# Attention scores of two groups in one step on eight 32x64 tiles, with a new order of the later steps

## The chip, the core and the metric

The kernel runs on one core of a Trainium2 chip. The metric is the device time of one execution in microseconds (us). Before the change three runs took 194.02, 194.83 and 199.41 us; the median, 194.83 us, is the time that counts. Every time below that is not one of these three comes from the profile of one execution of the same kernel.

## The reference

Inputs are q, k and v of 8 batches, 8 heads, 576 positions and head width 64, and four weight matrices. Attention is taken within chunks of 64 positions; a phase-mixing block follows on the concatenated heads:

```python
scores = scale * np.matmul(q_c, k_c.transpose(0, 1, 2, 4, 3))   # chunks of 64 x 64
attn = np.exp(scores - max); attn = attn / sum
x = np.matmul(attn, v_c)                       # (8, 576, 512) after the heads are joined
theta = x @ w_theta
zr, zi = x * np.cos(theta), x * np.sin(theta)
y = einsum('ts,bsd->btd', w_tok_r, zr) + einsum('ts,bsd->btd', w_tok_i, zi)
u = x + y
out = u + np.maximum(u @ w_ch, 0.0)
```

All arithmetic on the core is in fp16 operands with fp32 sums; inputs and the output in HBM are fp32.

## The kernel before, in words

**Work units.** The batches go in four pairs p = 0 to 3. A pair has nine tiles of 128 positions, j = 0 to 8: 0 to 3 of its first batch, 4 to 7 of its second, and tile 8 (MID), which joins the last 64 positions of both. For the attention the tiles are handled in groups: A (tiles 0, 1), B (2, 3), C (4, 5), D (6, 7) and M (tile 8).

**The order is a list written out by hand.** `ORDER` is a string of steps such as `S.2A.1`: the kind of step, then the pair and the group (or tile), then the slots or PSUM banks that it uses. A loop at the end of the kernel walks the list and calls one function for each step; every engine executes its own instructions in that order, and semaphores hold an instruction back until its inputs are there. So the list decides, for each engine and each DMA queue, what stands behind what.

**The kinds of step that matter here**, with the lines of the kernel before:

- `qk` (L167) loads q and k of a group, two DMAs of 256 KB on chip (L179; for M four of 64 KB, L174); `v` (L219) loads v of a group into `v16`, 256 KB in three DMAs (L233; M: 128 KB in two); `lw`, `lp`, `lc` load weights. All these are issued by GpSimd (POOL) in list order. They convert fp32 to fp16 on the way.
- `T` (L291) transposes q and k in 32x32 blocks on VectorE (L286).
- `S` (L334) makes the scores on TensorE: `score_mms` (L319) issues, for each of 8 heads, 2 halves e of the head width and 4 row quarters c, one matmul of 32 rows by 64 columns (L325): 64 for a full group, 32 for M, whose group has two quarters alone. A matmul works on one tile of the array: the quarter c gives its 32 rows, and the half `to` of the output gives its 64 columns. Of the eight such tiles a group uses four, one in each row quarter.
- `E` (L350) is the exponential on ScalarE, `V0`, `V1` (L376) the product with v for heads 0 to 3 and 4 to 7 on TensorE, in 64x64 tiles (L389): 16 matmuls for a full group, 8 for M. `N0`, `N1` (L398) divide by the sums on VectorE.
- `X` transposes x on TensorE (L421) and `xa`, `xv` copy the result; `xd` instead lets a DMA transpose x (L433). `H` is theta (L449), `G` cosine and sine on ScalarE, `Z` the products zr and zi on VectorE.
- `Y` is the token mix, nine matmuls of 128x128 by 512 for a tile (L528; for tile 8 eighteen in 128x64 tiles), `A` adds x, `U` with `ua`/`uv` or `ud` (DMA transpose, L563) turns u, `W` is the channel product (L573), `R` the relu and sum on VectorE (L578), and `st`, `sa`, `sg` store a tile of the output (256 KB) from the queue of SyncE (SP), ScalarE or GpSimd (L672). All `xd` and `ud` are issued by SP, in list order with the `st`.

**Where chunks lie.** The second tile of a group has its two chunks of 64 positions swapped in the partitions of v and of the exponentials (`crossed`, L215), except in groups A and B of pair 0. `load_v`, `score_mms` and `attn` all follow it. So the four score tiles of a group lie at column halves 0, 1, 1, 0 in the row quarters 0 to 3.

**Time around the change.** TensorE starts at 9.0 us, ends its last product at 187.7 us, and is seldom idle in between; loads are issued until 104.6 us, and the first transposing DMA and the first store are issued at 100.1 and 101.6 us.

Of the kernel before, what the change touches and what calls it, by code (L numbers as in the profile page):

```python
# [17 lines left out]
on.00 init.00 qk1.0A.0 pre.00 qk0.0A.1 qk.0B.2 cy0.0A.3 cv1.0A qk.0M.4 T0.0A.1 S0.0A.0 Tq.0B.0  # L18
v.0A Tk.0B v.0M v.0B Tq.0M.5 lw.03.2 S.0B.2 T1.0A E0.0A.0 V0.0A.0 Tk.0M S1.0A.4 E1.0A S.0M.6
lp.00 E.0M.1 V0.0M.7 N0.0A V1.0M.6 qk.0C.4 N1.0M V1.0A.4 dm.2.0 E.0B.2 lw.01.5 V1.0B.2 V0.0B.0  # L20
N1.0A X.0A.4 qk.1M.1 lw.02.3 N1.0B N0.0B xa.0A.1 X.0B.5 TW.03.3 v.0C N0.0M X.0M.7 xv.0B.2
H1.0A.5 G1.0A.0 H1.0B.0 G1.0B.3 xv.0M.4 Tq.0C.2 Z1.0A H0.0A.7 qk.0D.0 lw.00.6 G0.0A.1 v.0D
twv.03 Z0.0A H.0M.5 H0.0B.4 G.0M.4 TW.01.6 G0.0B.1 Ya.03.3 Tk.0C S.0C.0 Z1.0B twv.01 v.1M E.0C.3
Z0.0B Ya.01.6 Yb.01 TW.02.4 twa.02 Z.0M Ym.01 T.1M.2 A.01 Yb.03 V0.0C.0 Ym.03 V1.0C.4 Tq.0D.1
S.1M.6 E.1M.4 Ya.02.7 Yb.02 Ym.02 N1.0C Tk.0D S.0D.4 N0.0C A.03 TW.00.0 qk.1B.2 A.02 X.0C.3
lw.04.0 E.0D.3 U.01.6 ua.01.0 U.02.4 ua.02.1 U.03.5 twv.00 Ya.00.0 V1.0D.6 uv.03.2 qk.1A.6
xv.0C.1 N1.0D V0.0D.4 H.0C.2 G.0C.1 qk.1D.3 V0.1M.6 N0.0D X.0D.4 xv.0D.3 v.1B N0.1M Z.0C Yb.00
v.1A Ym.00 v.1D H.0D.4 Ya.05.2 T.1B.4 G.0D.5 V1.1M.3 A.00 Ya.06.6 TW.04.0 S.1B.4 Ya.04.7 N1.1M
X.1M.3 E.1B.4 Z.0D Yb.06 T.1A.4 Ym.06 S.1A.4 qk.1C.6 A.06 Yb.05 T.1D.5 xv.1M.3 U.06.6 twv.04
E.1A.1 Ym.05 Ya.07.4 V1.1B.0 qk.2M.3 A.05 ua.06.3 N1.1B V0.1B.5 N0.1B Yb.04 lc.00 S.1D.2 v.1C  # L30
V1.1A.0 Yb.07 qk.2C.5 Ym.07 qk.2D.4 N1.1A E.1D.2 V0.1D.2 N0.1D X.1B.0 xa.1B.4 V1.1D.5 Ym.04
H.1M.1 H.1B.2 qk.2B.0 N1.1D V0.1A.5 A.07 qk.2A.2 qk.3B.1 Y.08.4 T.1C.7 A.04 N0.1A X.1A.5 U.04.6
G.1M.2 Z.1M xv.1A.1 U.00.7 S.1C.0 v.2M G.1B.6 E.1C.4 A.08 X.1D.5 xv.1D.2 v.2B W.06.2 R.06.3
U.07.0 H.1A.4 uv.04.3 V0.1C.2 v.3D uv.07.4 v.2A uv.00.5 W.00.7 G.1A.7 N0.1C U.05.0 U.08.6
uv.08.5 v.2C V1.1C.2 W.01.1 uv.05.6 H.1D.4 N1.1C X.1C.2 Z.1A Z.1B R.01.2 qk.3A.6 W.08.3 xa.1C.4
Y.10.0 H.1C.1 G.1D.7 Z.1D T.2M.8 T.2A.7 W.02.4 S.2M.5 v.3B G.1C.9 Z.1C R.02.4 E.2M.1 Y.13.6 A.13
T.2B.9 S.2A.1 W.04.4 R.00.0 Y.16.5 qk.3D.0 R.04.5 R.08.6 W.05.4 S.2B.6 T.2D.7 E.2B.7 T.2C.2
Y.11.3 A.11 R.05.8 A.16 W.03.6 R.03.9 Y.15.7 A.15 E.2A.10 V1.2A.5 A.10 S.2C.3 E.2C.11 V0.2M.1
N0.2M V1.2M.7 N1.2M Y.14.2 N1.2A V0.2B.3 N0.2B V0.2A.0 V0.2C.6 v.2D Y.17.5 A.14 A.17 V1.2C.2
N1.2C N0.2A N0.2C Y.18.4 xd.2C.12 S.2D.2 st.04 qk.3M.2 V1.2B.0 E.2D.1 X.2A.5 W.07.6 N1.2B v.3C  # L40
V0.2D.0 R.07.7 N0.2D V1.2D.2 xa.2A.11 v.3A X.2M.7 X.2B.5 v.3M Y.12.6 A.12 N1.2D H.2A.0 xa.2M.10
A.18 T.3A.7 H.2M.6 xa.2B.1 G.2M.13 T.3D.5 Z.2M H.2C.4 H.2B.6 G.2A.6 xd.2D.5 ud.16.4 G.2C.0 Z.2C
ud.17.2 T.3B.9 H.2D.0 W.17.4 S.3D.2 G.2D.4 Z.2D ud.11.6 W.11.5 R.17.5 R.11.13 sa.06 ud.14.3
# [12 lines left out]
Y.33.4 A.33 st.15 ud.36.4 W.36.7 W.23.3 R.27.5 ud.38.2 sg.35 sa.34 R.23.13 R.36.1 W.38.6 R.38.0  # L56
sa.37 sa.28 Y.30.4 Wp.31.6.7 uv1.31 sa.38 A.30 W0.31 ud.32.3 W.32.1 R0.31.7 sa0.31 R.32.6 U.30.6
sa.36 W1.31 uv.30.1 R1.31 st.27 ud.33.6 W.33.4 R.33.0 st.32 sa.33 W.30.6 sg.23 dm.2.7 R.30.13
st1.31 sa.30
""".split()  # L60


@with_exitstack
def kernel(
# [11 lines left out]
    nc = tc.nc  # L76
    B, H, S, D = q.shape
# [670 lines left out]
```

## Time and profile before

| what | value |
|---|---|
| three timed runs | 194.02, 194.83, 199.41 us |
| span of the profiled execution, first to last instruction | 191.7 us |
| median of the runs less that span | 3.1 us |
| TensorE busy (matmul) | 173.9 us, 91% |
| TensorE weight loads | 91.1 us, 48% |
| VectorE busy | 138.8 us, 72% |
| ScalarE busy | 81.4 us, 42% |
| GpSimd busy (mostly issuing loads) | 88.4 us, 46% |
| DMA packets | 103338, 31.86 MB |

The profile gives the span of its execution and no other clock for it; what lies around the span is known only as the difference to the runs. A busy TensorE is not TensorE at its peak: matmuls overlap, so the record of one is longer than the time after which the next one starts. The chain of work that ended last gives the time from the start of a step to the start of the next; that is the price used below.

### The profile page before, as it was taken

Reading aid. Unit: us, or ns where it says so; the run is one execution under the profiler, and the core shown is the slowest. Engines: PE = TensorE matmul, PEld = TensorE weight load, DVE = VectorE, ACT = ScalarE, POOL = GpSimd, SP = SyncE. Lnnn points to the kernel's source line nnn. Section 1 sums busy time; section 2 is a strip of 40 time slices with the busy share of each in tenths; the row PEclk is TensorE's granted clock in tenths of the full one; section 3 lists DMA queues with packets and bytes.
Section 4 is the critical chain, followed back from the end, with each engine's and each line's share of the span. In section 5 each row is a group of like instructions: output and inputs, shape, how many; then the busy total and the mean of one; then the engine's idle time right before and its main releaser. Section 6 shows DMA issues by size and latency. Waiting matters only on the chain.

```text
span 191.7 us, 5957 instructions
## 1 busy us (share of the span) xinstructions
PE 173.9 (91%) x2579; PEld 91.1 (48%) x2579; DVE 138.8 (72%) x255; ACT 81.4 (42%) x100; POOL 88.4 (46%) x125
## 2 busy tenths in 40 slices
PE   0168899999999999999999969999999999999992
PEld 0155455645554655554555425454444444455450
DVE  0564789879779977996885968396686677553782
ACT  3113895476629946803218659142032560400000
POOL 8998289697798955799878000000000001100110
PEclk9999999999999999999999999999999999999999
DMA  5999999999999999999999986497356894885667
GB/s 159 202 157 182 188 132 143 164 177 165 151 153 183 175 182 181 157 116 152 164 133 132 196 145 168 82 197 222 74 158 126 112 281 103 246 230 150 180 173 259
DMA packets 103338, 31.86 MB, mean 166 GB/s; under 512 B 94672, under 2 KB 99152, under 8 KB 103312
## 3 DMA queue, kind: packets, MB, share of 16 engines
q0 software_dynamic: 76048, 17.33, 98.2%
q1 hardware_dynamic: 23872, 9.57, 23.9%
q10 hardware_dynamic: 3392, 4.59, 7.6%
q8 instruction: 20, 0.33, 0.7%
q14 instruction: 6, 0.05, 0.1%
HBM read 33.06 MB, written 9.44 MB: 222 GB/s over the span
## 4 chain that ended last, share of the span: by engine, by line
PE 78%; DMA 8%; DVE 4%; POOL 4%; issue 2%; ACT 1%; DVEq 0%; ACTq 0%; POOLq 0%
PE psum L528 35%; PE psum L573 14%; PE psum L449 12%; PE psum L325 6%; PE psum L389 5%; DMA out_dram<-mid 3%; PE psum L421 3%; DMA mid<-x 2%; DMA v<-in_v_dram 2%; PE psum L264 1%; POOL big L174 1%; PE psum L555 1%; POOL big L179 1%; DVE mid L578 1%; DVE x L406 1%
## 5 line engine op out<-in xcount | busy, mean ns | idle before, releaser
L528 PE MATMUL psum<-zr,wT 128*128 128x512 f16 (+2 forms) x185 | 62.6, 375 | 0.1
L528 PE MATMUL psum<-zi,wT 128*128 128x512 f16 (+2 forms) x184 | 59.6, 374 | 0.0
L528 PEld LDWEIGHTS <-wT 128*128 128x128 f16 (+1 forms) x369 | 31.3, 100 | 32.9 <-issue 0.5
L233 POOL DMA_DIRECT2D v<-in_v_dram x54 | 41.0, 787 | 10.1 <-DMA big<-in_k_dram 4.5
L672 POOL DMA_DIRECT2D out_dram<-mid x5 | 2.7, 551 | 75.3 <-DVE mid L578 75.3
L573 PE MATMUL psum<-wch,uT 128*128 128x512 f16 x140 | 35.1, 380 | 0.0
L550 DVE TENSOR_TENSOR x<-psum,x 128x512 f16<-128x512 f32 x35 | 23.7, 683 | 15.3 <-PE psum L528 15.1
L449 PE MATMUL psum<-wtheta,mid 128*128 128x512 f16 x144 | 33.2, 379 | 1.7 <-DMA mid<-x 1.7
L355 ACT ACTIVATE mid<-psum 128x1024 f16<-128x1024 f32 (+1 forms) x19 | 17.3, 930 | 33.9 <-PE psum L325 32.2
L578 DVE SCALAR_TENSOR_TENSOR mid<-psum,x 128x512 f32<-128x512 f32 (+1 forms) x37 | 23.9, 669 | 7.7 <-PE psum L573 5.6
L406 DVE TENSOR_TENSOR x<-psum,recip 128x512 f16<-128x512 f32 (+1 forms) x40 | 25.5, 638 | 1.4
L286 DVE STREAM_TRANSPOSE big<-big 128x1024 f32<-128x1024 f32 (+3 forms) x25 | 24.7, 1011 | 1.3 <-DMA big<-in_q_dram 0.9
L325 PE MATMUL psum<-big 32*64 32x64 f16 x1152 | 15.3, 199 | 9.5 <-DVE big L286 9.5
L471 ACT ACTIVATE big<-psum,pihalf 128x1024 f16<-128x1024 f32 x14 | 15.6, 1116 | 17.4 <-PE psum L449 17.4
L449 PEld LDWEIGHTS <-mid 128*128 128x128 f16 x144 | 13.9, 98 | 18.1 <-DMA mid<-x 2.2
L325 PEld LDWEIGHTS <-big 32*64 32x64 f16 x1152 | 13.0, 112 | 15.1 <-DVE big L286 10.1
L573 PEld LDWEIGHTS <-uT 128*128 128x128 f16 x140 | 12.4, 98 | 13.4 <-issue 0.8
L152 ACT ACT_TABLE_LOAD x12 | 15.4, 1283 | 6.3 <-DVE recip L404 4.8
L179 POOL DMA_DIRECT2D big<-in_q_dram x15 | 13.8, 920 | 1.7 <-DMA big<-in_k_dram 0.9
L472 ACT ACTIVATE big<-psum 128x1024 f16<-128x1024 f32 x14 | 14.3, 1024 | 0.0
L389 PEld LDWEIGHTS <-mid 64*64 64x64 f16 x576 | 8.9, 113 | 11.4 <-issue 9.0
L389 PE MATMUL psum<-v,mid 64*64 64x65 f16 x576 | 12.2, 202 | 2.0 <-DMA v<-in_v_dram 1.3
(51 smaller groups left out, 135.7 us busy)
## 6 DMA issues: line engine op xcount, KB each, us to landing
big<-in_q_dram POOLq DMA_DIRECT2D x15, 256.0 KB, 6.5
big<-in_k_dram POOLq DMA_DIRECT2D x15, 256.0 KB, 7.0
out_dram<-mid SPq DMA_DIRECT2D x13, 256.0 KB, 2.8
out_dram<-mid ACTq DMA_DIRECT2D x13, 256.0 KB, 3.0
v<-in_v_dram POOLq DMA_DIRECT2D x18, 128.0 KB, 5.7
v<-in_v_dram POOLq DMA_DIRECT2D x36, 64.0 KB, 6.1
out_dram<-mid POOLq DMA_DIRECT2D x5, 256.0 KB, 3.1
out_dram<-mid SPq DMA_DIRECT2D x5, 128.0 KB, 3.0
```

The costliest lines, as they stand in the source:

```text
L179: nc.gpsimd.dma_start(t[:, w].rearrange("p h s d -> p h (s d)"), ap[2 * p + bb, :, s0 : s0 + GT, :].rearrange("h (p s) d -> p h (s d)", s=2),)
L233: nc.gpsimd.dma_start(v16[rows, slot + t, :, 0:D], v[b, :, t0 : t0 + m, :].rearrange("h s d -> s h d"),)
L286: nc.vector.transpose(out.bitcast(FP32).rearrange("p (x l s) -> p x s l", l=32, s=2), in_.bitcast(FP32).rearrange("p (x s d) -> p x s d", ...
L325: nc.tensor.matmul(ps[half[to], r, h], t[quarter[c], 1, h, :, e], t[quarter[c], 0, h, :, e], start=(e == 0), stop=(e == 1), tile_position= ...
L355: nc.scalar.activation(out=eT[:, 0:n].rearrange("p r h i -> p (r h i)"), in_=st.pop(("ps_s", p, g)).rearrange("p r h i -> p (r h i)"), fun ...
L389: nc.tensor.matmul(ps[half[cc], r, h4, :], eT[rows, r, h, :], v16[rows, slot + r, h, 0 : D + 1],)
L406: nc.vector.tensor_tensor(out=x.rearrange("p r (h d) -> p r h d", h=HH), in0=ps[:, :, :, 0:D], in1=recip[:, 0:n].broadcast_to((P, n, HH, D ...
L449: nc.tensor.matmul(ps, xT[:, a, :], wtheta16[:, a, :], start=(a == 0), stop=(a == NDB - 1))
L528: nc.tensor.matmul(ps[half[b]] if j == MID else ps, w, z[:, cols], start=(kt == 0), stop=(kt == 2 * KT),)
L550: nc.vector.tensor_tensor(out=x, in0=st.pop(("ps_y", p, j)), in1=x, op=ALU.add)
L573: nc.tensor.matmul(ps, uT[:, a, :], wch16[:, a, :], start=(a == 0), stop=(a == NDB - 1))
L578: nc.vector.scalar_tensor_tensor(out=out, in0=ps, scalar=0.0, in1=x, op0=ALU.max, op1=ALU.add)
```

## The change

1. **Scores of two groups in one step.** `score_mms` takes a list of groups, and the innermost loop goes over them. A new step `SS` (`scores_of_two`) gives it two full groups: 128 matmuls instead of twice 64, those of the two groups in turn within each quarter. It stands four times in the list: pair 2 groups A and B, C and D; pair 3 groups C and D, A and B. Pairs 0 and 1 and all M keep `S`.
2. **The other four tiles for B and D.** `crossed` becomes `turned`: in groups B and D (apart from pair 0, group B) the first tile of the group is swapped instead of the second. Their score tiles then lie at column halves 1, 0, 0, 1, so that A with B, and C with D, use all eight 32x64 tiles. `load_v` loads the swapped tile in two pieces and the other in one, so the number and size of the v DMAs is as before; `attn` follows `turned`.
3. **A new order.** The list is the same up to the loads and scores of pair 0 but for the slots; from there most steps stand elsewhere. It has 558 steps instead of 562 (eight `S` became four `SS`). One `st` became an `sg`, one `uv` a `ua` and one `xv` an `xa`; the numbers of `xd`, `ud` and all other kinds are unchanged. Slots and banks are dealt anew.
4. Half steps take their slot when one is given, rather than when their half is the first; and the list may name two groups in a step. Neither adds an instruction.

The core of the diff:

```diff
-    def crossed(p, g):
-
-        return int(p > 0 or g not in "AB")
+    def turned(p, g, r):
+
+        if p == 0 and g in "AB":
+            return 0
+        return r ^ int(g in "BD")
...
-        elif not crossed(p, g):
-            parts = [(slice(0, P), t, 2 * p + bb, s0 + t * P, P) for t in range(2)]
         else:
-            parts = [
-                (slice(0, P), 0, 2 * p + bb, s0, P),
-                (half[1], 1, 2 * p + bb, s0 + P, CH),
-                (half[0], 1, 2 * p + bb, s0 + P + CH, CH),
-            ]
+            parts = []
+            for t in range(2):
+                t0 = s0 + t * P
+                if turned(p, g, t):
+                    parts += [(half[1 - i], t, 2 * p + bb, t0 + i * CH, CH) for i in range(2)]
+                else:
+                    parts.append((slice(0, P), t, 2 * p + bb, t0, P))
...
-    def score_mms(ps, t, n, heads, cross):
+    def score_mms(groups, n, heads):
         for h in range(heads):
             for e in range(2):
                 for c in range(2 * n):
-                    r, cc = (c // 2, c % 2) if n == 2 else (0, c)
-                    to = cc ^ (r * cross)
-                    nc.tensor.matmul(
+                    for p, g, ps, t in groups:
+                        r, cc = (c // 2, c % 2) if n == 2 else (0, c)
+                        to = cc ^ turned(p, g, r)
+                        nc.tensor.matmul(
...
+    def scores_of_two(p, gs, *bs):
+
+        score_mms([score_parts(p, g, b) for g, b in zip(gs, bs)], 2, H)
...
-                        rows = half[cc ^ (r * crossed(p, g))]
+                        rows = half[cc ^ turned(p, g, r)]
...
-        "S": scores, "E": exps, "V0": attn(0), "V1": attn(1), "N0": norm(0), "N1": norm(1),
+        "S": scores, "SS": scores_of_two, "E": exps, "V0": attn(0), "V1": attn(1), "N0": norm(0), "N1": norm(1),
```

Of the list two lines of the new one:

```
R.04.9 T.2A.11 A.13 Z.1C T.2M.18 W.08.5 R.06.12 SS.2AB.2.6 R.08.2 Z.1D Y.11.1 A.11 qk.2C.15 T.2C.0
E.2A.1 qk.3C.17 T.3C.1 v.2M Y.14.5 A.14 Y.15.0 A.15 W.05.3 qk.3A.4 R.05.3 E.2B.6 SS.2CD.6.1 S.2M.5
```

**Where instructions move: the loads of pairs 2 and 3 on POOL.** `big` holds q and k (rows of 128x8x128 are a full group, 32x8x128 a group M), `v_72` holds v. Before, from q and k of 3B to those of 3A; the third and second row from the end are v of group 2C:

```order
L179 DMA big<-in_q_dram 128x8x128
L179 DMA big<-in_k_dram 128x8x128
L233 DMA v_72<-in_v_dram 64x8x64 x2
L233 DMA v_72<-in_v_dram 128x8x64
L233 DMA v_72<-in_v_dram 64x8x64 x2
L233 DMA v_72<-in_v_dram 128x8x64
L233 DMA v_72<-in_v_dram 64x8x64 x2
L233 DMA v_72<-in_v_dram 128x8x64
L233 DMA v_72<-in_v_dram 64x8x64 x2
L233 DMA v_72<-in_v_dram 128x8x64
L233 DMA v_72<-in_v_dram 64x8x64 x2
L179 DMA big<-in_q_dram 128x8x128
```

Now, from q and k of 2M to those of 3M; v of 2C is again the third and second row from the end:

```order
L172 DMA big<-in_q_dram 32x8x128 x2
L172 DMA big<-in_k_dram 32x8x128 x2
L177 DMA big<-in_q_dram 128x8x128
L177 DMA big<-in_k_dram 128x8x128
L177 DMA big<-in_q_dram 128x8x128
L177 DMA big<-in_k_dram 128x8x128
L233 DMA v_72<-in_v_dram 64x8x64 x2
L177 DMA big<-in_q_dram 128x8x128
L177 DMA big<-in_k_dram 128x8x128
L233 DMA v_72<-in_v_dram 128x8x64
L233 DMA v_72<-in_v_dram 64x8x64 x2
L172 DMA big<-in_q_dram 32x8x128 x2
```

The q and k of 2C, 3C and 3A now stand right ahead of v of 2C. Counted over the whole queue, v of 2C has one full q and k group and one v group more ahead of it than before: 3C and 3A came ahead of it and 3B went behind it, and v of 2D came ahead.

**The start of SP's queue.** `x` to `mid` is an `xd`, `x` to `uT` a `ud`, `mid` to `out_dram` a store. Before:

```order
L193 DMA big<-in_q_dram 128x4x128 x2
L433 DMA_TRANSPOSE mid<-x 128x8x128
L672 DMA out_dram<-mid 128x512
L433 DMA_TRANSPOSE mid<-x 128x8x128
L563 DMA_TRANSPOSE uT<-x 128x4x128 x4
```

Now:

```order
L191 DMA big<-in_q_dram 128x4x128 x2
L680 DMA out_dram<-mid 128x512
L677 DMA out_dram<-mid 64x512 x2
L571 DMA_TRANSPOSE uT<-x 128x4x128 x3
L441 DMA_TRANSPOSE mid<-x 128x8x128
L571 DMA_TRANSPOSE uT<-x 128x4x128
L680 DMA out_dram<-mid 128x512
```

The first `xd`, of group 2C, now has two stores (tiles 7 and 8 of pair 0) and three `ud` (tiles 5, 4 and 3 of pair 1) ahead of it; none of these waits for anything of pair 2.

More of the change, by code (lines that the diff above doesn't have):

```diff
@@ L24 @@
[L24 to L29, printed above, removed]
@@ L653, in step @@
         def step(p, j, slot=None):
-            if f == 0:
+            if slot is not None:
                 st["o", p, j] = mid(slot, 1, FP32)
```

106 lines of the change are left out of this document (55 added, 51 removed).

## The prediction

> **What bounds the kernel now.** I read the page first: the busy line, the slices, the shares of the chain.
>
> ```profile
> span 191.7 us, 5957 instructions
> PE 173.9 (91%) x2579; PEld 91.1 (48%) x2579; DVE 138.8 (72%) x255; ACT 81.4 (42%) x100; POOL 88.4 (46%) x125
> PE   0168899999999999999999969999999999999992
> DMA  5999999999999999999999986497356894885667
> PE 78%; DMA 8%; DVE 4%; POOL 4%; issue 2%; ACT 1%; DVEq 0%; ACTq 0%; POOLq 0%
> ```
>
> TensorE (PE) carries 78% of the chain and is busy in nearly every slice. The DMA row is the second thing to see: 9 in every slice but the first up to slice 23, which is 110 us. So for the first 110 us two resources are full at once. Next, what PE waits for, and both resources in one stretch (columns: length, PE with its count, PEld, DVE, ACT, POOL, clock, DMA share, GB/s).
>
> ```profile
> PE psum L325 <- DVE big L286: 9.5, 2, 9.0
> PE psum L449 <- DMA mid<-x: 1.7, 1, 1.7
> PE psum L389 <- DMA v<-in_v_dram: 1.3, 2, 0.7
> 66.00:103.00 37.00, 37.00 (x644) 19.37 (x642) 31.17 (x56) 15.80 (x19) 28.66 (x40) 1.00 1.92 153
> ```
>
> The 9.5 us are the start, before any scores exist. After it PE loses almost nothing: 1.7 us for a DMA transpose, 1.3 us for v. From 66 to 103 us it never idles, at full clock, while the DMA engines' packets overlap to 1.92 times their number: a saturated load stream under a saturated PE. The old order just fits the two together, so PE work that is taken out ahead of a load gains only if that load is early enough.
>
> **What a step costs on PE.** From the chain in order of time (start, length, what), some pieces:
>
> ```profile
> 20.11 0.62 PE psum L421 x8
> 91.20 0.64 PE psum L325 x59
> 92.22 2.05 PE psum L528 x9
> 94.26 0.51 PE psum L389 x48
> 96.82 0.25 PE psum L389 x16
> 97.07 2.06 PE psum L528 x18
> 100.58 0.86 PE psum L573 x4
> 123.32 0.64 PE psum L325 x64
> 123.96 0.97 PE psum L573 x4
> 124.93 1.94 PE psum L528 x9
> 126.87 0.62 PE psum L325 x32
> 127.75 0.73 PE psum L325 x63
> 136.28 0.24 PE psum L389 x8
> ```
>
> A matmul of 512 columns takes 1.94 / 9 = 0.216 us. A step in another tile shape than the step ahead of it takes 0.10 to 0.12 us more: Y 2.05 behind V against 1.94 behind W; W 0.97 behind S against 0.86 behind X; the first V 0.25, but three V in a row 0.51, so 0.13 for each further one. I price a change of shape at 0.10 us. Then S is 0.54, V 0.14, Y of a tile 8 1.96 without it.
>
> **The eight tiles.** S of a group M (32 matmuls, two tiles) takes 0.62 us, S of a full group (64, four tiles) 0.64. So the pace is that of one tile doing its 16 matmuls, and the number of tiles at work is nearly free. Eight tiles would give SS 0.64 us instead of 1.28: the low bound. What speaks for more is the row at 127.75: at the end of a run of 112 small matmuls without a long one between, S took 0.73, as if instructions came too slowly; all of SS at that pace, 11.4 ns a matmul, is 1.46 us: the high bound, worse than two S. I take 0.85, the tile's pace and twice the 0.09 us that the dense run lost; it is nearer to the low bound since that row is from the same kind of matmul, and the S at 91.20 and 123.32 show no loss. Whether two tiles in the same rows can work at once is a separate doubt. V answers it for 64x64 tiles: V of a full group puts two tiles in each half of the rows, V of M one, and they take 0.25 and 0.24.
>
> The Trainium skill has a rule that speaks against this (TensorE: Matmul & The Clock Gate, Part 3, The mechanism): a weight load overlaps a running matmul only when its row group differs. By it SS would stay at 1.28 us. The V rows disagree; no run here shows it for 32x64 tiles.
>
> **PE work, part by part.** I split the program where V0 of group 2C starts (94.5 us now, the third V in the row at 94.26), because there the new order meets a load. Counts are from the two lists.
>
> *From 20.1 us (X of 0B, the same in both lists) to V0 of 2C:* 74.4 us now. Changes of shape: 48 become 29, -1.9. Y of tiles 10 and 16 go behind the split, W of 07 and Y of 18 come ahead: -14 x 0.216 + 1.96 = -1.1. One V of 16 and two of 8 go behind: -0.4. Three S (1.62) become two SS (2 x 0.75 without the change): -0.1. Sum -3.5: PE alone could be at V0 of 2C at 91.0.
>
> *From there to the end of the last W* (187.55, the start of the dummies, below): 93.05 us now. Changes of shape 33 to 20, -1.3. The moved Y, W and V come back, +1.1 and +0.4. Five S become two SS: 1.5 - 2.7 = -1.2. The wait of 1.7 us goes: its `xd` (2D) gets work ahead of it. Sum -2.7, which leaves 90.3. Against that I set 0.3 us at one place, where the scores of 3C and 3D come behind theta of 2B. ScalarE's groups:
>
> ```profile
> L471 ACT ACTIVATE big<-psum,pihalf 128x1024 f16<-128x1024 f32 x14 | 15.6, 1116 | 17.4 <-PE psum L449 17.4
> L472 ACT ACTIVATE big<-psum 128x1024 f16<-128x1024 f32 x14 | 14.3, 1024 | 0.0
> L152 ACT ACT_TABLE_LOAD x12 | 15.4, 1283 | 6.3 <-DVE recip L404 4.8
> L355 ACT ACTIVATE mid<-psum 128x1024 f16<-128x1024 f32 (+1 forms) x19 | 17.3, 930 | 33.9 <-PE psum L325 32.2
> ```
>
> Between theta of 2B and V1 of 3D, ScalarE must run cosine, sine, a table load and two exponentials: 1.12 + 1.02 + 1.28 + 2 x 0.93 = 5.3 us and the handovers. PE has two Y, a W, SS and a V there, 5.9 us: the cover is about as long as the work.
>
> **The loads decide when PE reaches V0 of 2C.** POOL's rows, then what the DMAs issued in 82.9 to 84.5 and in 103.6 to 104 us took to land (name, queue, count, KB each, us):
>
> ```profile
> 35.02 0.89 POOL L179 DMA_DIRECT2D big<-in_q_dram  x1 [0.87 <-DMA big<-in_k_dram]
> 79.26 5.16 POOL L233 DMA_DIRECT2D v<-in_v_dram  x7 [0.86 <-PE psum L325]
> 103.69 0.95 POOL L179 DMA_DIRECT2D big<-in_k_dram  x1
> ```
>
> ```profile
> v<-in_v_dram POOLq DMA_DIRECT2D x2, 64.0 KB, 4.2
> big<-in_k_dram POOLq DMA_DIRECT2D x1, 256.0 KB, 7.5
> ```
>
> v of 2C is the last three of the seven, so its last piece is issued at 83.6 and lands at 87.8; now it is used at 94.5, 6.7 us later. q and k of 1B, issued from 35.0, land about 7 us on, at 42.0. In the 45.8 us between, 8.5 groups of q and k (512 KB on chip), 8.5 of v (256 KB), the channel weights (512 KB) and 144 KB of token weights land: 7184 KB, 157 KB per us. In the new order a q and k group and a v group more stand ahead of v of 2C: 768 KB, 4.9 us. It lands at 92.7 if nothing else uses the DMA engines.
>
> But something does. Before, the first transposes and stores came at 100 us (SP's queue):
>
> ```profile
> 100.10 1.43 SPq L433 DMA_TRANSPOSE mid<-x  x1
> 101.58 0.75 SPq L672 DMA_DIRECT2D out_dram<-mid  x1
> 107.49 1.24 SPq L433 DMA_TRANSPOSE mid<-x  x1
> ```
>
> What that costs the loads can be worked out. From 87.8 to the last landing at 111.2 (103.69 + 7.5) 2944 KB of loads came; at 157 KB per us that is 18.8 us, and it took 23.4. The 4.6 us more go with two or three times 256 KB of transposes and a store: 1.5 to 2.3 us for each. In the new order two stores (256 KB each) and two or three `ud` (128 KB each) are issued ahead of that landing, the `ud` perhaps too late to count fully: 0 us if they only use gaps, 1.5 x 2 to 2.3 x 3.5 = 3.0 to 8.1 if they displace loads. I take 2.8, just under the low end, since stores are few large packets and the `ud` come within the last 4 us. So v of 2C lands at 95.5, and V0 of 2C starts at 95.6 instead of 94.5: **later than now**, although PE has 3.5 us less to do. Behind it on PE stand Y of 16 and all the rest. Earlier waits of the same kind (v of 1D moves behind the channel weights and q and k of 1C) are swallowed by this one, and so is the gain of the first two SS.
>
> **The end.** The last rows of PE and of the store queue:
>
> ```profile
> 187.55 0.59 PE L163 MATMUL psum<-zeros 128*128 128x512 f16 x2
> 188.02 0.94 ACTq L672 DMA_DIRECT2D out_dram<-mid  x2
> ```
>
> ```profile
> out_dram<-mid ACTq DMA_DIRECT2D x2, 256.0 KB, 4.3
> out_dram<-mid ACTq DMA_DIRECT2D x2, 256.0 KB, 2.1
> ```
>
> From the end of W to the end of the span are 4.1 us now. Stores alone land in 2.1 us (the last two, issued at 188), three issued within 1 us in 4.3 (those at 174.7): 0.7 us more for each that queues. The new list holds stores back: 12 tiles are stored in about the last 7 us of PE work, 8.4 us at 0.7 each, so up to 1.4 us late. I take half: 4.8.
>
> **Sum** against the profiled execution's span: 95.6 + 90.3 + 0.3 + 4.8 = 191.0, which is 0.7 less than 191.7. The median of the runs lies 3.1 above that span, so I forecast 194.83 - 0.7 = **194.1 us**: no change that can be told (2%, 3.9 us, is about what a measurement of this kernel can tell). Its own range, with contention 1.0 to 4.0 us, SS 0.64 to 1.1, the end 4.1 to 5.5: 191.2 to 196.5.
>
> **Rivals.**
>
> *The load is in time* (faster). If transposes and stores fill gaps, v of 2C lands at 92.7, PE arrives there at about the same time, and the new order's lighter PE work counts: 92.8 + 90.3 + 4.3 = 187.4, so 190.5 us; with SS at 0.64 and the small waits gone 189.5. For it: a load's landing varied, and two stores are a small part of 7 MB. Against it: a DMA row of 9s has no gaps to fill. Chance 0.25.
>
> *The load is later still* (slower). At 2.3 us for each 256 KB v of 2C lands at 92.7 + 8.1 = 100.8; then 100.9 + 90.3 + 0.3 + 4.8 = 196.3, which gives 199.4 us. It decides as soon as the landing is past 96.2, where my sum is even. For it: the DMA share of 1.92; against it: the `ud` come late. At 1.9 us and three times 256 KB it is 197.0. Chance 0.18.
>
> *The eight tiles do not do what the change says.* If tiles in the same rows take turns, SS is 1.28; the two behind the split cost 0.86 more, the two ahead are hidden in the wait: 195.0 us, no change either. Starved at 1.46 it is 195.3. Chance 0.15.
>
> **How the numbers follow.** My forecast has 0.42, the rivals 0.25, 0.18 and 0.15. Faster by over 2% means below 190.9: most of the first rival and a little of the forecast, 0.23. Slower by over 2% means above 198.7: half of the second, with a bit for a wait that I have not seen in a list so much changed, 0.11. Within 2%: 0.66. The likeliest is 194.1. The range for 8 in 10 goes from 189.6 to 198.0: it cuts off the best of the first rival and the worst of the second.
>
> **What would show it.** Right: in the new profile V0 of 2C waits for `v<-in_v_dram`, 2 us or more, at about 95 us, in a stretch that PE now passes without idle time; SS takes 0.8 to 0.9 us for 128 matmuls; PE's busy time is less by some 4 us while the span is not; the wait of L449 for `mid<-x` is gone or small. Wrong: no wait for v beyond 60 us and a last W that ends before 184 (first rival); that wait at 98 or later (second); L325 of SS at 1.2 us or more (third). A wait of over 2 us anywhere behind V0 of 2C would show that I have missed a chain in the new order.

## The result and the profile after

The changed kernel takes **207.88 us** (median of 4 runs, 206.39 to 208.47) against 194.57 us of the kernel before in the same session (4 runs, 194.02 to 199.41). The ratio is 1.068, 95% interval 1.061 to 1.075: **slower by 7%**, where 194.1 us, no change that can be told, was forecast. Some executions of a kernel are slow, 2% or so longer, as the one of 199.41 us; the ratios and intervals here and below leave them out, the medians do not. The profiled execution took 208.3 us, its span is 206.5.

The page of the changed kernel, the rows that answer to those of before (busy time, slices, granted clock, chain):

```profile
span 206.5 us, 5924 instructions
PE 177.2 (86%) x2579; PEld 93.7 (45%) x2579; DVE 137.2 (66%) x253; ACT 79.9 (39%) x98; POOL 89.8 (43%) x127
PE   0158999899999999968997739999999999999950
PEclk9999999999999999995899967999999999999998
DMA  6999999999999999999999991116646713347995
PE 68%; DMA 16%; POOL 8%; issue 3%; DVE 1%; ACT 1%; ACTq 0%; DVEq 0%; POOLq 0%
```

Three things are new. PE's row has two holes, at slices 17 to 18 and 21 to 23 (of 5.2 us each, counted from 0). The granted clock falls in both or just behind, which it never did between 19 us and the end before. And the DMA row stays at 9 to slice 23, that is to 124 us instead of 110. PE's busy time went up by 3.3 us although it changes its tile shape less often; work at half clock, 13.7 us of it, takes longer.

What PE waits for, over the whole span (total, times, longest):

```profile
PE psum L326 <- DVE big L286: 9.3, 2, 8.4
PE psum L457 <- ACT big L480: 4.5, 1, 4.5
PE psum L326 <- issue: 2.9, 2, 2.7
PE psum L397 <- DMA v<-in_v_dram: 1.5, 2, 0.8
PE psum L457 <- DMA mid<-x: 1.2, 1, 1.2
PE psum L581 <- DMA uT<-x: 1.1, 1, 1.1
```

The first row is the start, as before. The second is theta of 2D (`H.2D`), the third a pause inside `SS.2CD` for which no engine and no DMA is named ("issue"). v, on which the forecast rested, costs no more than before. The two stalls in the chain of waits (start, length, what):

```profile
89.19 0.86 PE psum L581 x4
90.06 1.07 PE psum L326 x116
91.13 2.65 issue
93.78 1.13 PE psum L326 x42
94.91 3.98 PE psum L536 x17
...
107.76 0.88 PE psum L457 x4
108.64 10.87 DMA mid<-x
...
119.58 0.36 ACTq L680
...
121.00 1.02 ACT big L480
122.03 0.04 issue
122.07 3.57 PE psum L457 x8
```

Behind each stall the same work takes twice its price: Y of tile 18 takes 3.98 us (1.96 in the prediction's prices), eight matmuls of theta 3.57 us (8 x 0.216 = 1.73). The windows say why (columns as in the prediction: length, PE, PEld, DVE, ACT, POOL, clock, DMA share, GB/s):

```profile
92.60:99.40 6.80, 5.62 (x106) 3.00 (x110) 0.64 (x3) 3.91 (x5) 5.11 (x7) 0.50 2.25 150
99.40:104.00 4.60, 4.60 (x74) 2.19 (x62) 4.43 (x12) 0.00 (x0) 3.49 (x5) 0.99 1.76 174
119.90:126.80 6.90, 4.73 (x12) 1.71 (x12) 2.58 (x4) 5.07 (x6) 0.00 (x0) 0.51 0.78 221
126.80:133.00 6.20, 6.20 (x153) 3.25 (x152) 4.91 (x7) 4.99 (x6) 0.00 (x0) 1.00 0.02 9
```

The clock is at half for 6.8 us from within each stall on (it falls at 92.6 and 119.9 us), and at full speed again from one row to the next.

**Where the 15.5 us between forecast (191.0) and span (206.5) lie.** Each step's start on PE in the trace, less the prices of the prediction, gives: V0 of 2C starts at 99.3 us instead of 95.6 (+3.7); from there to the end of the last W, at 199.5, it takes 100.2 us instead of 90.6 (+9.6); the end takes 7.0 us instead of 4.8 (+2.2).

### The profile page after: what moved, and what is told of

Read it like the earlier page. It is cut to its first block, busy times and chain, and to the rows that moved or that the text cites. A ratio compares the mean times of both kernels' runs of the same rounds, so it can differ in the third digit from the quotient of the medians.

```text
span 206.5 us, 5924 instructions
## 1 busy us (share of the span) xinstructions
PE 177.2 (86%) x2579; PEld 93.7 (45%) x2579; DVE 137.2 (66%) x253; ACT 79.9 (39%) x98; POOL 89.8 (43%) x127
## 4 chain that ended last, share of the span: by engine, by line
PE 68%; DMA 16%; POOL 8%; issue 3%; DVE 1%; ACT 1%; ACTq 0%; DVEq 0%; POOLq 0%
PE psum L536 32%; PE psum L581 13%; PE psum L457 12%; DMA big<-in_k_dram 8%; DMA mid<-x 5%; PE psum L326 4%; POOL v L233 4%; PE psum L397 3%; DMA uT<-x 3%; POOL big L177 2%; PE psum L429 2%; POOL big L172 1%; PE psum L563 1%; POOL big L243 1%; PE psum L264 1%
## 5 line engine op out<-in xcount | busy, mean ns | idle before, releaser
L536 PE MATMUL psum<-zr,wT 128*128 128x512 f16 (+2 forms) x185 | 63.3, 387 | 0.0
L536 PE MATMUL psum<-zi,wT 128*128 128x512 f16 (+2 forms) x184 | 60.7, 387 | 0.0
L536 PEld LDWEIGHTS <-wT 128*128 128x128 f16 (+1 forms) x369 | 32.0, 103 | 34.2 <-issue 2.6
L457 PE MATMUL psum<-wtheta,mid 128*128 128x512 f16 x144 | 34.7, 393 | 5.6 <-ACT big L480 4.5
L581 PE MATMUL psum<-wch,uT 128*128 128x512 f16 x140 | 34.3, 385 | 1.1 <-DMA uT<-x 1.1
L286 DVE STREAM_TRANSPOSE big<-big 128x1024 f32<-128x1024 f32 (+3 forms) x25 | 25.2, 1019 | 5.5 <-DMA big<-in_q_dram 2.7
L581 PEld LDWEIGHTS <-uT 128*128 128x128 f16 x140 | 13.2, 99 | 16.1 <-DMA uT<-x 1.6
L506 DVE TENSOR_TENSOR zr<-x,big 128x1024 f16<-128x1024 f16 x14 | 9.5, 680 | 10.7 <-ACT big L479 10.7
L412 DVE RECIPROCAL recip<-psum 128x8 f32<-128x8 f32 (+1 forms) x40 | 7.8, 194 | 12.6 <-PE psum L397 12.5
L177 POOL DMA_DIRECT2D big<-in_q_dram x15 | 13.7, 913 | 2.9 <-DMA big<-in_k_dram 1.7
```

What stands on the lines that cost most here:

```text
L177: nc.gpsimd.dma_start(t[:, w].rearrange("p h s d -> p h (s d)"), ap[2 * p + bb, :, s0 : s0 + GT, :].rearrange("h (p s) d -> p h (s d)", s=2),)
L286: nc.vector.transpose(out.bitcast(FP32).rearrange("p (x l s) -> p x s l", l=32, s=2), in_.bitcast(FP32).rearrange("p (x s d) -> p x s d", ...
L457: nc.tensor.matmul(ps, xT[:, a, :], wtheta16[:, a, :], start=(a == 0), stop=(a == NDB - 1))
L536: nc.tensor.matmul(ps[half[b]] if j == MID else ps, w, z[:, cols], start=(kt == 0), stop=(kt == 2 * KT),)
L581: nc.tensor.matmul(ps, uT[:, a, :], wch16[:, a, :], start=(a == 0), stop=(a == NDB - 1))
```

## Theories for the two stalls

*First stall.* **Theory 1**: the eight tiles take instructions faster than they come; SS is the fault. The trace's records show that there is something in it: in SS.2AB the first 32 matmuls start in waves of eight, most of them 32 ns apart (so all eight tiles do work at once; if the two in a row quarter took turns, a wave would need twice that), and then, when what was queued is used up, exactly one every 8.33 ns, 4.17 ns for each instruction. SS so takes 1.17 us.

**Theory 2**: PE's instructions come from memory in blocks, and the block that holds the end of SS.2CD came late. The page counts them:

```profile
q8 instruction: 20, 0.33, 0.6%
```

20 packets of 16 KB for 5158 weight loads and matmuls: 258 instructions a block. Counted over the whole program, the pause is ahead of instruction 3009, which is 193 + 11 x 256; 193 is simply the remainder that turns up here, and the experiments show whether it comes back. A block's packet goes from 91.3 to 92.2 us, and PE takes up work at 93.8. The one before went at 84.5, the next two at 97.6 and 104.3: in this stretch of full DMA engines 6.3 to 6.8 us from one to the next. PE's work in the block ahead of the pause, from 87.1 to 90.9 us, was 3.8 us long; 3.8 and the 2.9 of the pause are 6.7. So in this stretch a block that PE uses up in less than some 6.5 us makes it wait, if no earlier slack is left. The windows of after and of before, 82 to 92 us, show the density (the second number is PE's with its count):

```profile
82.00:92.00 10.00, 9.13 (x276) 5.09 (x275) 7.97 (x12) 2.76 (x4) 7.98 (x11) 1.00 1.63 172
```

```profile
82.00:92.00 10.00, 10.00 (x197) 5.07 (x196) 8.47 (x12) 1.98 (x3) 9.77 (x13) 1.00 2.02 138
```

276 matmuls against 197 in the same time. Before, PE took 6.8, 6.0 and 7.5 us for the three blocks from 78.9 to 99.2 us: what a transfer takes here. But 6.5 us is no fixed price of full DMA engines: the block behind these, from 99.1 us, was used up in 3.3 us, the packet of the next one went 3.9 us after the one before it, and PE paused for 0.2 us only.

The Trainium skill (Runtime: NRT & Kernel Launch, Instruction fetch mechanics) describes such blocks: 16 KiB or 256 instructions, the next one fetched while the current one runs, "mostly hidden" since the sequencer needs about 20 cycles for an instruction. The size agrees with these records. That it stays hidden does not: the pace was 4.17 ns an instruction, and the next block came 6.7 us behind the one before.

*Second stall.* Theta of 2D needs its x, from a DMA transpose (`xd.2D`), and the PSUM banks of theta of 2C, which cosine and sine of 2C must have read. **Theory 3**: the transpose is what is late, since it goes through full DMA engines: 10.87 us in the chain above. The DMA transposes issued from 104 to 121 us after, and then from 100 to 121 us before (name, queue, count, us to landing):

```profile
uT<-x SPq DMA_TRANSPOSE x6, 6.6
mid<-x SPq DMA_TRANSPOSE x2, 9.1
```

```profile
uT<-x SPq DMA_TRANSPOSE x8, 2.9
mid<-x SPq DMA_TRANSPOSE x2, 5.4
```

**Theory 3a**: the store of tile 14 makes it worse. ScalarE's rows:

```profile
111.54 1.01 ACT L449 COPY mid<-psum 128x1024 f16<-128x1024 f16 x1 [1.65 <-PE psum L429]
119.58 0.36 ACTq L680 DMA_DIRECT2D out_dram<-mid  x1
119.99 1.11 ACT L479 ACTIVATE big<-psum,pihalf 128x1024 f16<-128x1024 f32 x1 [7.44 <-DMA mid<-x]
```

ScalarE does nothing for 7.4 us; cosine of 2C stands behind the store, and the store waits for a transpose with which it has nothing to do. The two lists of instructions tell why (row number of the engine's list, and the semaphores waited for):

```
ACT 73 L680 DMA out_dram<-mid 128x512 [waits DMAHW5_49,DVE_49]
ACT 74 L479 ACTIVATE big<-psum,pihalf 128x1024 [waits PE_49]
SP  11 L441 DMA_TRANSPOSE mid<-x 128x8x128 [waits DVE_49,DMAHW5_49,PE_49,Activation_49]
```

Stores and transposes share eight completion semaphores; the store of tile 14 got the one that `xd.2D` raises (number 116 for both in the trace), and must let that landing come first.

**Theory 4**: the half clock is a consequence of the stalls, with a price of its own.

## Experiments

All times are medians of 4 runs (e8: 10) beside runs of the kernel before on the same chip; the ratio is to that kernel. "e3" and so on name them.

### e1: each SS as two S

```diff
-SS.2AB.2.6          (and 2CD, 3CD, 3AB)
+S.2A.2 S.2B.6
```

> Each of the four steps SS is written as two steps S in the same place, same tiles, same banks; nothing else moves. Theory 1 (SS is the fault: eight tiles take instructions faster than they come, PE's queue is empty when the stall comes): two S need 0.64 us each, just the pace of the instructions, the queue stays full, the stall of 2.9 us at 91 us and the half clock behind it go: 207.9 - 2.9 - 2.3 = about 202.5 us. Theory 2 (the block of 256 instructions that holds the rest of SS.2CD comes late from DRAM because its transfer stands behind the loads; what counts is how many instructions PE uses in how short a time): two S have the same 256 instructions and last only 0.1 us longer, the stall stays at 2.5 to 2.9 us: 207 to 209 us.

**206.1 us** (204.5 to 209.5), ratio 1.052 (1.041 to 1.064). The stall in the chain of waits:

```profile
93.08 1.10 PE psum L326 x114
94.18 2.88 issue
97.06 1.10 PE psum L326 x28
```

It is as long as with SS and ahead of the same instruction, 3009. Theory 1 falls, as far as this stall goes. The time is a little under what theory 2 gave, as the wait of theta of 2D is 1.7 us here instead of 4.5 (everything ahead of it came later, in part since the clock was also at half for 3.4 us at 38.7 us, far ahead of the edit; the traces of e5 and e12 show the same); its interval touches that of the changed kernel.

### e2: the ends of the blocks moved

```diff
-qk1.0A.0 pre.00
+qk1.0A.0 pre.00 dn.58.7        # 58 matmuls of 32x8 on zeros
```

> 58 very short matmuls on zeros (8 columns, 116 instructions) are added at 3 us, where PE has nothing to do until 8.4 us; all the rest is as in the changed kernel, only each block of 256 instructions now ends 116 instructions earlier in the program. Theory 2 (late instruction blocks): the ends fall in the middle of SS.2AB and of SS.2CD, and between them lie some 7 us of long matmuls instead of the two ends within 0.6 us of queue room; a block that takes 5.6 us to come is in time, the stall at 91 us is under 0.5 us and the clock does not fall there: 207.9 - 2.7 - 2.3 = about 203 us. Theory 1 (SS itself empties the queue) or any wait of PE on data: the stall stays where it is, 207 to 209 us. The added matmuls may also raise the clock a little earlier than 21.0 us, at most 1 us of gain.

**205.8 us**, ratio 1.054 (1.045 to 1.063). There is no pause inside SS.2CD any more, so it depended on where the block ends, not on SS or on data. But the time fell by 2 us only: the pauses turned up at other ends of blocks. All pauses of PE over 0.5 us between 60 and 112 us, read from the trace's records in the order of the program, for some of the kernels:

```
kernel          ahead of instruction (n = 193 + 256 k)   pause, ns
before          none
after           3009 (k 11)                              2860
e1              1985, 2241, 2753, 3009                   572, 746, 600, 3070
e2              2241, 3265                               1317, 1590
e3              1985, 3009                               710, 2598
e6              1985, 2753, 3265                         654, 625, 2302
e7              3009, 3265                               789, 1570
```

Pauses for data are left out of this table (in e2 1.1 us at 94.3 for an addition of VectorE, in e3 1.9 us at 111.8 for a transpose). Of those over 0.8 us for which no engine and no DMA is named, each stands at such a number. 3009, 3265 and 2241 are different steps in these kernels; what they share is the place in the block. The old order has such pauses too, only shorter: 0.3 us ahead of 1985 in the kernel before, and 0.8 and 0.5 us in e10 and e9, at the end of the block where the kernel before has its 0.2 us.

### e3: x of 2D turned on PE

```diff
-st.05 xd.2D.4 Z.2C
+st.05 X.2D.2 xv.2D.4 Z.2C
```

> x of group 2D is turned on PE (8 matmuls, 0.86 us, and a copy on VectorE) instead of by the DMA transpose that took 10.9 us; nothing else moves. Theory 3 (the second stall, 4.6 us before theta of 2D, comes from the transpose that goes through full DMA engines, and the half clock behind it from the stall): the store of tile 14 on ScalarE no longer stands behind that transpose, theta of 2D waits at most 1 us, the clock stays full there: 207.9 - 3.6 - 2.3 = about 202 us. Rival (another wait takes its place, since theta of 2D needs the PSUM banks of theta of 2C, and cosine of 2C stands behind the store): the wait stays over 3 us and now names ScalarE alone: 207 us or more.

**200.9 us**, ratio 1.029 (1.021 to 1.038): 7.0 us less than the changed kernel. Theory 3 holds. Some 1.4 us of the gain is there ahead of theta of 2C already (its transpose is issued at 103.9 us instead of 105.3), since the first stall and its half clock were shorter in this execution; about 6 us belong to the edit. What PE waits for from 60 to 126 us:

```profile
PE psum L326 <- issue: 2.9, 2, 2.4
PE psum L457 <- DMA mid<-x: 1.7, 1, 1.7
```

Theta of 2D no longer waits; theta of 2C waits 1.7 us for the other transpose, which took 7.9 us. The clock was at half for 3.4 us in the middle of the program instead of 13.7.

### e4: the wait filled

```diff
-R.16.13 H.2D.0
+R.16.13 dm.16.2 H.2D.0         # 16 matmuls of 512 columns on zeros
```

> 16 matmuls of 512 columns on zeros (3.5 us at full clock) are put on PE just ahead of theta of 2D, into the 4.6 us in which PE waits there; they compute nothing. Theory 4 (the clock falls to half because PE stood idle, and that costs 2.3 us in theta of 2D and W of 17 behind it): with 1.2 us of idle time left the clock stays full from 99.4 us on, and the time falls by 2 to 2.5 us to about 205.5. Rival (the clock falls for another reason, or what PE does at half clock is covered by other waits): no change, 207.4 to 208.5.

**203.2 us**, ratio 1.044 (1.032 to 1.056): 4.7 us less for work that computes nothing. The clock row of its page:

```profile
PEclk9999999999999999999999999999999999999996
```

The clock never fell between its rise and the end, and theory 4 holds: theta of 2D and what follows it, to the end of theta of 2B, take 4.5 us here and 6.8 in the changed kernel, so the clock costs the 2.3 us expected. The other half of the gain is not the edit's. PE starts W of 14, ahead of the added work, at 104.1 us instead of 106.9, mainly since the clock did not fall behind the first stall either (2.4 us here instead of 2.9). The length of the stall alone does not explain that: in e11 a stall of 2.8 us at the same place left the clock at full as well. With neither cost in the way, the load of the forecast comes into sight:

```profile
PE psum L397 <- DMA v<-in_v_dram: 0.2, 1, 0.2
```

PE reaches V0 of 2C at 95.3 us, waits for v and goes on at 95.6, the time that the forecast gave.

### e5: the store moved

```diff
-H.2A.4 sa.14 T.3A.7 G.2C.8 ... G.2D.13 Z.2D
+H.2A.4 T.3A.7 G.2C.8 ... G.2D.13 sa.14 Z.2D
```

> The store of tile 14 on ScalarE's queue, which stood ahead of cosine of 2C, is issued behind cosine and sine of 2D; nothing else moves. Theory 3a (the store is half of the second stall: it may go only when the DMA transpose of 2D has landed, at 119.5 us, and cosine of 2C stands behind it, so theta of 2D gets its banks 2.5 us after its x is there): theta of 2D starts when the transpose lands, its wait is 2.1 us instead of 4.6, and the clock stays full: 207.9 - 2.5 - 2.3 = about 203 us. Rival (the transpose alone sets it): the wait stays at 4 us or more, 207 us or more.

**204.3 us**, ratio 1.049 (1.043 to 1.056), 3.6 us less. From 60 to 126 us PE waits for instructions only:

```profile
PE psum L326 <- issue: 3.8, 2, 2.8
PE psum L397 <- issue: 0.8, 1, 0.8
```

The wait of theta of 2D is gone, more than the 2.5 us of theory 3a: with the first stall and a later start the transpose, 6.9 us long here, was in time. How much of that is the store's, e1 tells: there W of 14 starts at 110.5 us as here, the transpose lands at 119.0 (119.3 here), and with the store in its old place theta of 2D starts at 121.6 us instead of 119.9. So the store alone made PE wait 1.7 us there. How the 4.5 us of the changed kernel would split with the earlier start is not shown.

### e6: two Y ahead of SS.2CD (on e3)

```diff
-E.2B.6 SS.2CD.6.1 S.2M.5 E.2C.0 Y.18.3 V1.2A.6 ... V0.2C.4 Y.16.2 N1.2D
+E.2B.6 Y.16.5 A.16 Y.18.3 SS.2CD.6.1 S.2M.5 E.2C.0 V1.2A.6 ... V0.2C.4 N1.2D
```

> On the version with x of 2D turned on PE (200.9 us): Y of tiles 16 and 18 (27 matmuls, 3.9 us, 54 instructions) stand ahead of SS.2CD instead of behind it. Theory 2 (the block that holds the end of SS.2CD comes some 11 us after PE's instructions ran into SS.2AB, two transfers of 5.6 us one after the other): PE gets to the end of that block some 3.5 us later than the 2.6 us that it waited, so the stall is under 0.5 us and the clock stays full: 200.9 - 2.6 - 1.4 = about 197 us. Rival (the stall belongs to SS.2CD and goes with it): it is still 2 us or more, 200 to 202 us. A wait for exponentials or for v of 2C may take up to 1.5 us of the gain, since those come no earlier.

**202.2 us**, ratio 1.039 (1.032 to 1.046); e3 has 200.9. The pause in SS.2CD is gone, as expected, and the time is not: 2.3 us now ahead of instruction 3265, inside V1 of 2M. The two Y had been what covered the transfer of the next block. I had asked only whether the block in question had time, not what the next one would lack.

### e7: fewer loads

```diff
         st["qk", p, g] = t
+        if p == 3 and g in "AC":
+            return
         for w, ap in enumerate((q, k)):
```

> q and k of groups 3A and 3C are not loaded (1 MB of the load stream, some 6.5 us of it, from 84 us on; their scores are made from what stands in the buffers), TensorE's program is the same instruction by instruction. Theory 2 (instruction blocks wait behind the loads): the block transfers after 84 us start 1 to 3 us after they are asked for instead of 5 to 8, the stall inside SS.2CD is under 1 us; with that, its half clock and shorter transposes for theta of 2D the time is 200 us or less. Rival (the block transfers are slow for a reason of their own): the stall stays at 2.5 us or more; the transposes may still gain, 203 to 206 us.

**202.1 us**, ratio 1.029 (1.021 to 1.037). The pause ahead of 3009, with the same instructions of PE, is 0.8 us instead of 2.9; the packets of these blocks went at 83.6 and 88.3 us, 4.7 us apart instead of 6.8. That is theory 2's part: fewer loads, a shorter pause. The loads are not shown to be all of it. I had expected packets 1 to 3 us after they are asked for (counted as in the last point of this document); the packet of 88.3 us still went 6.5 us after that, instead of 8.3, when the DMA engines came free at 88.2. The trace is of the slowest of four runs, 202.9 us. The total of 200 us or less was missed by all but one run, of 199.5. What PE waits for, and ScalarE ahead of it:

```profile
PE psum L459 <- DMA out_dram<-mid: 3.9, 1, 3.9
PE psum L399 <- issue: 1.4, 1, 1.4
```

```profile
113.69 0.36 ACTq L682 DMA_DIRECT2D out_dram<-mid  x1
114.10 1.11 ACT L481 ACTIVATE big<-psum,pihalf 128x1024 f16<-128x1024 f32 x1 [5.54 <-DMA mid<-x]
```

The next block still came late (1.6 us), and the store still stood ahead of cosine until the transpose landed, 8.5 us after its issue, although the last load had landed at 111.3 us instead of 120.8.

### e8: the shape of the step alone

```diff
 (order of the kernel before, code of the change)
-S.2A.1 W.04.4 ... S.2B.6
+W.04.4 ... SS.2AB.1.6
```

> The order of the kernel before with the changed code: scores turned by half a tile as in the change, and one SS for 2A and 2B at the place of S of 2B (S of 2A is gone from its old place); nothing else moves. If the form of the step is neutral (SS 1.17 us for two S of 0.64 and a change of shape less): 194.4 to 194.8 us. If a step of 256 instructions by itself makes PE wait for a block (theory 1): 2 to 3 us more, 196.5 to 198 us. The low price of the prediction, 0.64 to 0.85 us, would give 194.0.

**194.9 us** beside 194.8, ratio 1.0015 (0.998 to 1.005). The SS in its chain:

```profile
85.75 1.17 PE psum L328 x127
```

The tiles turned by a half and a step of 256 instructions cost nothing and bring nothing that can be told, for this one of the four SS. With e1, where all four are taken apart in the new order and nearly all of the loss stays, this puts the loss on the order.

### e9 and e10: 256 instructions more in the kernel before, early and late

```diff
-R.00.0 Y.16.5               (e9, at 82 us)       -Y.34.7              (e10, at 160 us)
+R.00.0 dn.128.5 Y.16.5                           +dn.128.7 Y.34.7
```

> The kernel before, with 128 very short matmuls on zeros (8 columns, 256 instructions: one block more) ahead of Y of 16, at about 82 us, in the stretch of full DMA engines; they compute nothing. By themselves they take some 1.7 us of PE (the 58 of the shifted kernel took 1.5 us at half clock, 26 ns each, so 13 ns at full clock). Theory 2 (a block takes some 6 us to come while the loads run, whatever PE does with its instructions): the block more is worth 3 to 6 us of stall on top, at places where PE waits for nothing else: 199.5 to 202.5 us. Rival (only the eight-tile steps or the new order make PE wait): 1.7 us in all, 196.0 to 197.0 us.

> The same 128 matmuls in the kernel before, ahead of Y of 34, at about 160 us, where the DMA engines are mostly free. Both theories: a block comes within 2 us here and long matmuls stand on both sides, so they cost their own 1.7 us or a little more: 196.0 to 197.5 us. Over 199 us would speak against theory 2, since the blocks would then cost the same without loads.

**201.5 us** (1.032, 1.027 to 1.038) and **201.9 us** (1.029, 1.023 to 1.035). They tell nothing apart. The added matmuls took twice what I had priced (start, length in e10):

```profile
156.87 3.35 PE L163 MATMUL psum<-zeros 128*32 128x8 f16 x128
```

26 ns each, on one and the same tile, and a block of 3.3 us with long matmuls on both sides is no dense stretch: no pause for a block followed in e9. Both also had 3.4 us at half clock: e9 at 120.0 us, behind a wait of 2.1 us for a transpose, e10 just behind the added matmuls:

```profile
161.30:164.70 3.40, 3.40 (x10) 1.22 (x9) 0.00 (x0) 0.00 (x0) 0.00 (x0) 0.53 0.12 41
```

By the words I had put down, over 199 us late speaks against theory 2. It would, if the excess were waits for blocks; in the execution that was traced, of 199.6 us, 5.0 over the kernel before, it is 3.3 us of matmuls and 1.7 us lost to the clock, and nothing is left.

### e11: seven stores earlier (on e3)

```diff
 sa.00 sa.02 st.17 st.18 st.22 sa.25 st.28 each moved
-(in the last 20 us of the list)
+(behind sa.13, sa.12, st.01, Z.3D, A.34, A.34, Y.35)
```

> On the version with x of 2D turned on PE (200.9 us): the stores of tiles 00, 02, 17, 18, 22, 25 and 28 are issued 15 to 60 us earlier in their queues, at 125 to 165 us, instead of in the last 20 us. Theory 5 (the 7.0 us between the last matmul and the end are stores that queue, 5.4 us from issue to landing where single ones take 2.3): the last ones land in 2.5 to 3.5 us, and the transposes of the last tiles, 5 us long there, come sooner: 200.9 - 2.5 to 3.5 = about 198 us. Rival (the end is set by the last tiles' own chain, or the earlier stores stop ScalarE or SP as the one of tile 14 did): 200 to 202 us or more.

**200.3 us**, ratio 1.027 (1.021 to 1.033), against 200.9: no gain that can be told. W of 33 and 37 no longer wait for their transpose, but the last store still landed 6.0 us after the last matmul of W, as in the changed kernel. Nine stores are issued in its last 2.9 us (191.1 to 194.0); it is these that queue, not the older ones.

### e12: Y of 17 earlier too (on e6)

```diff
-V0.2C.4 N1.2D A.18 ... N1.2C Y.17.3 st.08
+V0.2C.4 A.18 Y.17.3 N1.2D ... N1.2C st.08
```

> On the version with Y of 16 and 18 ahead of SS.2CD (202.2 us, where PE waits 2.3 us for the next block of instructions, inside V1 of 2M): Y of tile 17 (9 matmuls, 1.9 us) also stands earlier, ahead of V0 and V1 of 2M; nothing else moves. Theory 2 in its second form (every block takes some 6.5 us from one to the next in this stretch, so a block that PE could use up in less makes it wait, wherever that block ends; the blocks after it hold long matmuls and have time to spare): PE gets to the end of the block 1.9 us later, the wait there is 0.4 us, and the clock is at half for 3.4 us at most: 202.2 - 1.9 - 1 = about 199 us. Rival (the wait goes on to the next dense step again, or exponentials and copies that now come in another order replace it): a wait of over 1.5 us at the next end of a block or elsewhere before 112 us, 201 to 203 us.

**203.4 us**, ratio 1.043 (1.034 to 1.052); not better than e6. The pause ahead of 3265 is 0.3 us instead of 2.3, as theory 2 had it (the row for L536 below is another, ahead of 2753). The rival's second half came true for the time. PE from 84 to 107 us:

```profile
PE psum L397 <- ACT mid L363: 1.2, 2, 0.6
PE psum L397 <- DVE x L414: 0.8, 2, 0.5
PE psum L536 <- issue: 0.3, 1, 0.3
```

V now waits for exponentials and divisions. Three long steps moved ahead of the dense ones leave nothing behind them that could cover ScalarE and VectorE. No version here beats the kernel before.

## Why the prediction was wrong, point by point

- *PE and loads are both full for the first 110 us.* Right, and it is the ground of all that followed. But I drew only one consequence, that v of 2C would be late. Full DMA engines also carry PE's own instructions and the transposes, and neither had a term in the sum. This is the step that failed: the sum let PE's instructions come for nothing, and it let the transpose of 2D cost what it had cost before.
- *v of 2C lands at 95.5 us, V0 of 2C starts at 95.6.* The load was right: its last piece landed at 96.3. The step failed all the same, because PE got there at 99.3 and did not wait for v. Of the 8.3 us between "PE alone at 91.0" and 99.3 the trace gives 2.9 to the pause, 2.2 to the half clock behind it and 0.6 to two SS; a rest of 2.6 I have not placed singly (the clock rose at 21.0 us instead of 18.7, and there are small waits before 60 us). Without the pause and its clock V0 would have met v at 96.4; in e4 it did, at 95.6.
- *SS takes 0.85 us, bounds 0.64 and 1.46.* Measured 1.17: inside the bounds, 0.32 too low. The tile's pace was read rightly: in the traces S of a group M starts two matmuls every 32 ns, S of a full group four every 33, and SS its first waves of eight every 32. What I priced too low is the pace of the instructions. Four matmuls in 33 ns are 8.3 ns each, and 8.33 ns is also the fastest at which matmuls with their weight loads come once what was queued is used up. So eight tiles gain only on what stands ready, and the rest of SS goes at the pace of four. The rule of the Trainium skill (TensorE: Matmul & The Clock Gate, Part 3, The mechanism), that a weight load overlaps a running matmul only when its row group differs, would have given 1.28 by the prediction's working. That number is nearer, but the trace does not agree with the rule: eight tiles, two in each row group, start together as long as instructions are queued.
- *81 changes of shape become 49, worth 3.2 us.* Not contradicted by any run, but never measured alone: it is lost among the stalls.
- *"The wait of 1.7 us goes: its `xd` (2D) gets work ahead of it."* **This is the step that failed worst.** Work ahead of it on PE does not help when the transpose itself takes 10.9 us instead of 4.7, in a stretch where the loads run on to 120.8 us and SP issues its transposes and stores one behind the other. How much each of these adds is not shown: in e7, with the last load at 111.3 us, it still took 8.5. The wait became 4.5 us, and 2.3 us of half clock came behind it. I had worked out that transposes delay loads and not that a transpose among them takes longer itself. e3 shows this part to be worth about 6 of its 7.0 us; e5 takes the wait away by moving one store, which I had passed over as it stood behind nothing on PE, and is 3.6 us faster.
- *0.3 us for exponentials at SS.3CD.* No such wait came.
- *The end takes 4.8 us.* It took 7.0. I had worked out 1.4 us for stores held back and took half; the whole and more was due, because the last twelve are issued in 6.0 us, and the last three land 5.4 to 5.6 us after their issue.
- *The rivals.* Break-even at 96.2 us for the load: it landed there, so by that mechanism alone the time would have been even. The sentence that a wait of over 2 us behind V0 of 2C would mean a missed chain was the one that came true; its chance, "a bit" of 0.11, was too small for a list so much changed.

The three misses, 3.7, 9.6 and 2.2 us, are so in the main: the two stalls with their clock (5.1 and 6.8), four SS (1.3 in all), theta of 2C and W of 37 waiting for their transposes (1.2 and 1.1), the end (2.2) and the rest of 2.6 ahead of V0 of 2C; less the 4.6 us that the forecast had PE wait for v anyway (from 91.0 to 95.6), and the 0.3 at SS.3CD. **Shown** by runs are the second stall and its two causes, transpose and store (e3, and e5 beside e1), the price of the clock behind it (e4), the place of the first stall in the block (e1, e2, e6, e12), that fewer loads shorten it (e7), and that the shape of the step is neutral (e8 for one SS, e1 for the four). **Open** is why the blocks' packets come later in the new order than in the old, where the DMA engines are as full; how they are ranked against the loads' there is not seen, only their times.

## What to carry to other kernels

Where the DMA engines are full, count PE's instructions per time and not only its work: a run of small matmuls uses up 256 instructions in 1 to 4 us, and under load the next block came up to 6.8 us behind the one before. Price a transpose or store that is moved into such a stretch by its own latency there, and look at what stands behind a store on the engine that issues it, down to the semaphore that it shares. And reckon, with each expected stall of PE of 2 us or more, that the clock may fall as well: 6.8 us at half clock cost 2.2 and 2.3 us here.

## What the runs showed of the hardware that I had not expected

- The length of a pause alone does not tell whether the clock falls. By the records of the first stall (from start to start) it fell behind 2.6 us (e3, for 3.4 us), within 2.9 us (the changed kernel, for 6.8 us, 1.5 us after PE's last matmul), and not at all with 2.4 us (e4) and 2.8 us (e11). In e6 it fell 1.1 us ahead of the pause, behind two waits of 0.6 us among small matmuls.
- It changes in steps. Between its first rise and its last fall, every stretch at full or at half clock in these traces is a whole multiple of 3.41 us: 71.68, 6.83 and 20.48 us in the changed kernel are 21, 2 and 6 of them. Where a stall lies against these steps may be what decides; no run tests that.
- It also fell behind 3.4 us of back-to-back matmuls of 8 columns (e10), in which PE counts as busy 3.40 of 3.40 us, and did not fall behind the same matmuls in e9 (84.9 to 88.2 us). So it is not idle time by the profile's reading alone that decides.
- Instructions come at 4.17 ns each, 8.33 ns for a weight load with its matmul, once what was queued is used up. Matmuls of one and the same tile follow each other every 26 ns with 8 columns (e10) and every 32 ns with 64 (S of a group M).
- A packet of PE's instructions starts 1.1 to 1.2 us after PE's records come within 64 instructions of the end of a block where the DMA engines are free (three blocks from 131 to 142 us), and 4.8 to 8.3 us after it where they are full (six blocks from 68 to 114 us). In the kernel before, the six packets from 69 to 106 us, where its DMA engines are full as well, start 2.9 to 4.9 us after it.
